# A fused attention, token-mixer and MLP kernel: the second batch's edges go, one rotation moves behind the first token unit, and the residual's transposing transfers lead

## The chip, the cores and the metric

One core of one Trainium2 chip runs the whole program. The metric is device time of one execution in microseconds (us). TensorE is the matrix engine, VectorE, ScalarE and GpSimd work on tiles in SBUF, and SyncE issues most of the transfers (DMAs). Each engine, and SyncE's queue with it, takes its instructions in the order in which they stand in the program; an instruction that waits holds up all that is behind it on its engine.

## The reference

Eight batches of 576 tokens and 512 channels (8 heads of 64) pass through three stages. Cut to what matters:

```python
kv  = einsum('bhsd,bhse->bhde', k, v)                 # per head, 64x64
out = einsum('bhsd,bhde->bhse', q, kv)
x   = out / sqrt(mean(out*out, -1) + 1e-6) * g_norm   # (B, S, 512)

theta = x @ w_theta                                   # rotation
y = w_tok_r @ (x * cos(theta)) + w_tok_i @ (x * sin(theta))
u = x + y
u = u + relu(u @ w_ch)

h = relu(u.T @ w_tok1) @ w_tok2                       # over tokens
u = u + h.T
return u + relu(u @ w_ch1) @ w_ch2                    # MLP, 1536 wide
```

## The kernel before

**Stages.** Every float32 product is made of three float16 products (`mm3`, L103 to L105): each operand is a high part and the low part that is left over. A batch's 576 tokens are five tiles, the last one of 64. For a batch the work is: `kv` (K units), `attend` (five a units, one a tile: product with q, square, sum, power on GpSimd, scaling to x, split into two halves xs, transposing transfer to xt, residual R), `rotate` (five r units: product with w_theta into pt, range reduction, sine and cosine, product with x into cs, split into zh and zl; the fifth, `rotate_last`, works the other way round and turns its result zt into the last two rows of zh by a transposing transfer, L450), `mix` (M00 to M03 for the first 256 token columns, M10 to M13 for the other 320; 27 matmuls each, the last three of which need zh's last two rows), `channel` (C00 to C13; after each second one a transposing transfer xt<-xs, L514), `token1` (H00, H01 on the first column chunk's xt; H10, H11 on the second's) and `token2` (T00 to T13). A K, a or r unit belongs to the next batch or the one after it, and is issued beside the M, C, H and T units of the current one. The second half of the program is the MLP over all batches, in eight pieces; its wide weights are decoded and prepared beside the batches (`stash`).

**What sets the order.** A list of names, `STEADY`, is the order of a batch's main units; a dictionary, `BESIDE`, says after which of them each r, a, load or weight unit is issued ("M12": "r2" issues the third tile's rotation after M12). A unit is a generator: `go` first steps every open unit by one `yield`, then starts the new one, so a unit's later operations stand in the program behind those of the units issued since. From this program order a scheduler makes each engine's order; it may move an instruction ahead where it counts the engine free. The helpers `lead` and `placed` (L77 and L81) limit it: `lead` notes the last instruction of a main unit on its engine, and `placed` adds an edge without a semaphore, so that a side operation does not stand ahead of the last noted one. `beside(o)` gives `placed` for every batch but the first, whose rotation has `early` (a higher priority) instead. So the attention of the second batch, issued beside the first batch's M units, stands on VectorE and ScalarE behind the evictions of those units (L476, L477). `decode` places its three VectorE operations likewise, also while the first batch is prepared.

Tile names: py is a mix product in PSUM, R the residual, uh and ul its halves, pr a channel product, ph a token product, pu its second, po an attention product, ss and ri the sum and its power. Two tiles of the name xs are shared by the halves xs and the last rotation's zt. There are 8 PSUM banks.

Of the kernel before, what the change touches and what calls it, by code (L numbers as in the profile page):

```python
# [14 lines left out]
ALU = mybir.AluOpType  # L15
# [13 lines left out]
def attn_mixer_kernel(  # L29
# [4 lines left out]
    nc = tc.nc  # L34
# [104 lines left out]
    wp = []  # L139

    def decode(val, raw):

        bits = val.bitcast(I32)
        first = nc.scalar.activation(val, raw[..., 1].bitcast(F32), AF.Copy, scale=2.0**-112)
        if wp:

            tc.keep_in_program_order(first)
        yield
        placed(nc.vector.tensor_scalar(bits, bits, 3, None, ALU.logical_shift_left))
        placed(nc.vector.scalar_tensor_tensor(bits, raw[..., 0], 29, bits, ALU.logical_shift_right, ALU.bitwise_or))  # L150
        placed(nc.vector.scalar_tensor_tensor(bits, raw[..., 1], -(2**31), bits, ALU.bitwise_and, ALU.bitwise_or))

    def weight(pool, w, src, part, n, hi, lo, scale, name, raw=None):

# [156 lines left out]
    def attend(o, r):  # L311

        b = o.b
        if r == 0:
            o.R = mp.tile([P, KD, S], F32, tag="R", name=f"R{b}", bufs=2)
            o.x, o.xt = {}, {}
        po = bank(f"po{b}{r}")
        for hp in range(HP):
            nc.tensor.matmul(po[:, hp * P:(hp + 1) * P], o.q[:, hp, r * P:(r + 1) * P], kvbd[:, hp, :], start=True, stop=True)
        po3 = po.rearrange("p (h d) -> p h d", d=D)  # L320
        ss = fp.tile([P, H], F32, tag="ss", name=f"ss{b}{r}", bufs=3)
        ri = fp.tile([P, H], F32, tag="ri", name=f"ri{b}{r}", bufs=3)
# [12 lines left out]
        nc.gpsimd.tensor_tensor(
            x3, ri.unsqueeze(2).to_broadcast([P, H, D]), gb.unsqueeze(1).to_broadcast([P, H, D]), ALU.mult
        )
        yield
        yield
        place(nc.vector.tensor_tensor(x3, po3, x3, ALU.mult))  # L340
        n = SR if r == NR else P
        R = o.R[:, :, r * P:r * P + n]
        if b == 0:

            yield
            px = bank(f"px{r}").rearrange("p (k t) -> p k t", k=KD)
            for kk in range(KD):
                nc.tensor.transpose(px[:, kk, :], x[:, kk * P:(kk + 1) * P], ident)
            yield
            split(xt[:, 0], xt[:, 1], px, 1.0)  # L350
            nc.scalar.activation(R, px[:, :, :n], AF.Copy, scale=SW)
            return
        if b > 1:
            yield
        place(nc.scalar.activation(xs[:, 0, :], x, AF.Copy))
        yield
        place(nc.vector.tensor_tensor(xs[:, 1, :], x, xs[:, 0, :], ALU.subtract))
        nc.sync.dma_start_transpose(xt.rearrange("p a k t -> p (a k) t"), xs.rearrange("p a d -> p (a d)"))
        for _ in range(3 if b > 1 else 2):
            yield  # L360
        place(nc.scalar.activation(R, xt[:, 0, :, :n], AF.Copy, scale=SW))
        yield
        place(nc.vector.scalar_tensor_tensor(R, xt[:, 1, :, :n], SW, R, ALU.mult, ALU.add))

    def beside(o):
        return placed if o.b else lambda ins: ins

    def prepare(o):
        if o.zh is None:
# [42 lines left out]
    def rotate_last(o, xt):  # L412
# [69 lines left out]
    def channel(o, c, ct):  # L482
# [25 lines left out]
        with urgent():  # L508
# [284 lines left out]
    def run(units, o, nxt, after, also):  # L793
# [23 lines left out]
    TOKENS1 = ["K00", "H00", "H01", "K10", "H10", "H11"]  # L817
    STEADY = MIX[:6] + CHANNEL[:2] + MIX[6:] + CHANNEL[2:4] + ["K00"] + CHANNEL[4:] + TOKENS1[1:] + TOKEN2
    BESIDE = {
        "M00": "a2", "M01": "a3", "M02": "a4 l w", "M03": "r0", "M11": "r1", "M12": "r2",  # L820
        "C03": "r4", "C10": "w", "H01": "r3 w", "H11": "n0", "T01": "n1 w", "T12": "w",
    }
    for b in range(B):
        loaded.clear()
# [23 lines left out]
        elif b == 1:  # L848
# [90 lines left out]
```

## Time and profile before

| what | value |
|---|---|
| time before, median of 3 runs | 1122.71 us (1122.53 to 1125.02) |
| the profiled execution, its own time | 1125.0 us |
| its span | 1123.2 us (1.8 us lie around it) |
| TensorE busy | 1072.1 us (95%) |
| TensorE weight loads busy | 814.7 us (73%) |
| VectorE / ScalarE / GpSimd busy | 829.7 / 560.1 / 229.3 us |
| TensorE's granted clock, mean | 0.983 |

The clock is a share of 2.4 GHz: 1.00 is that, 0.50 is 1.2 GHz. The timeline views list what each engine did, with the idle time before it and what ended that; SPq rows are issues of transfers on SyncE's queue. The first batch's own mixing ends near 116 us, the batches end at 625 us, and the rest is the MLP. One steady batch takes 71 to 74 us: the fourth (counted from zero, batch 3) has its H units at 344 to 360 us.

### The profile page before, as it was taken

Reading aid. Unit: us, or ns where it says so; the run is one execution under the profiler, and the core shown is the slowest. Engines: PE = TensorE matmul, PEld = TensorE weight load, DVE = VectorE, ACT = ScalarE, POOL = GpSimd, SP = SyncE. Lnnn points to the kernel's source line nnn. Section 1 sums busy time; section 2 is a strip of 40 time slices with the busy share of each in tenths; the row PEclk is TensorE's granted clock in tenths of the full one; section 3 lists DMA queues with packets and bytes.
Section 4 is the critical chain, followed back from the end, with each engine's and each line's share of the span. In section 5 each row is a group of like instructions: output and inputs, shape, how many; then the busy total and the mean of one; then the engine's idle time right before and its main releaser. Section 6 shows DMA issues by size and latency. Waiting matters only on the chain.

```text
span 1123.2 us, 21650 instructions
## 1 busy us (share of the span) xinstructions
PE 1072.1 (95%) x8884; PEld 814.7 (73%) x8884; DVE 829.7 (74%) x1475; ACT 560.1 (50%) x958; POOL 229.3 (20%) x290
## 2 busy tenths in 40 slices
PE   4786999999998999999999999999999999999998
PEld 3473767776875777667777777777777777777776
DVE  4978868888886987978836485858677585858584
ACT  3755635556455364564622454636364544546361
POOL 2405034372641925628000000000000000000000
PEclk9887999999998999999999999999999999999999
DMA  9535456875747647664284702020110102020101
GB/s 315 211 107 131 97 160 151 217 191 135 215 123 207 189 123 201 169 153 110 48 272 81 285 12 75 1 78 9 38 48 28 59 12 75 12 75 1 44 1 43
DMA packets 146611, 126.35 MB, mean 112 GB/s; under 512 B 93200, under 2 KB 123024, under 8 KB 146512
## 3 DMA queue, kind: packets, MB, share of 16 engines
q1 hardware_dynamic: 141136, 104.53, 34.0%
q0 software_dynamic: 5376, 20.45, 5.1%
q8 instruction: 69, 1.13, 0.4%
q14 instruction: 30, 0.25, 0.1%
HBM read 74.29 MB, written 29.88 MB: 93 GB/s over the span
## 4 chain that ended last, share of the span: by engine, by line
PE 61%; DVE 18%; DMA 8%; ACT 5%; issue 4%; POOL 3%; SPq 0%; ACTq 0%; DVEq 0%; POOLq 0%
PE na L103 4%; PE na L105 4%; PE pa L104 4%; PE pa L105 4%; PE na L104 4%; PE pa L103 4%; DMA xt<-xs 4%; DVE cs L403 2%; PE py L105 2%; PE py L103 2%; PE py L104 2%; PE nc L105 2%; PE pc L104 2%; PE pc L105 2%; PE pc L103 2%
## 5 line engine op out<-in xcount | busy, mean ns | idle before, releaser
L103 PE MATMUL py<-wmh,zh 128*128 128x320 f16 (+1 forms) x576 | 165.3, 287 | 0.7 <-DMA zh<-zt 0.5
L104 PE MATMUL py<-wml,zh 128*128 128x320 f16 (+1 forms) x576 | 165.0, 287 | 0.0
L105 PE MATMUL py<-wmh,zl 128*128 128x320 f16 (+1 forms) x512 | 146.5, 287 | 1.9 <-DVE zl L410 1.9
L105 PE MATMUL na<-gh,wbl 128*128 128x288 f16 x384 | 109.4, 286 | 0.0
L104 PE MATMUL pa<-o,wah 128*128 128x288 f16 x384 | 109.3, 286 | 0.0
L104 PE MATMUL na<-gl,wbh 128*128 128x288 f16 x384 | 109.2, 286 | 0.0
L103 PE MATMUL pa<-o,wah 128*128 128x288 f16 x384 | 108.4, 286 | 0.0
L105 PE MATMUL pa<-o,wal 128*128 128x288 f16 x384 | 107.8, 286 | 0.0
L103 PE MATMUL na<-gh,wbh 128*128 128x288 f16 x384 | 106.1, 286 | 0.2
L620 DVE TENSOR_TENSOR gl<-sum,gh 128x1152 f16<-128x1152 f32 x48 | 64.9, 1353 | 21.9 <-ACT gh L619 21.9
L104 PEld LDWEIGHTS <-wbh 128*128 128x128 f16 x672 | 65.7, 98 | 17.7 <-issue 0.9
L103 PEld LDWEIGHTS <-wah 128*128 128x128 f16 x672 | 65.7, 98 | 16.6
L104 PEld LDWEIGHTS <-wah 128*128 128x128 f16 x672 | 65.7, 98 | 16.6
L105 PEld LDWEIGHTS <-wbl 128*128 128x128 f16 x672 | 65.7, 98 | 16.6
L103 PEld LDWEIGHTS <-wbh 128*128 128x128 f16 x672 | 65.7, 98 | 16.6
L105 PEld LDWEIGHTS <-wal 128*128 128x128 f16 x672 | 65.7, 98 | 16.6
L334 POOL TENSOR_TENSOR ri<-ss,mhalf 128x8 f32<-128x8 f32 x40 | 76.8, 1920 | 1.6
L103 PE MATMUL pr<-uh,wch 128*128 128x256 f16 (+1 forms) x256 | 73.1, 286 | 0.0
L105 PE MATMUL pr<-uh,wcl 128*128 128x256 f16 (+1 forms) x256 | 73.0, 286 | 0.0
L104 PE MATMUL pr<-ul,wch 128*128 128x256 f16 (+1 forms) x256 | 73.0, 286 | 0.0
L103 PEld LDWEIGHTS <-zh 128*128 128x128 f16 x576 | 56.6, 98 | 16.8 <-DMA zh<-zt 0.9
L619 ACT ACTIVATE gh<-sum 128x1152 f16<-128x1152 f32 x48 | 55.5, 1156 | 25.5 <-DVE sum L667 25.5
(292 smaller groups left out, 2905.3 us busy)
## 6 DMA issues: line engine op xcount, KB each, us to landing
c<-u2d SPq DMA_DIRECT2D x32, 288.0 KB, 4.2
out<-c SPq DMA_DIRECT2D x64, 144.0 KB, 1.8
q<-in_q SPq DMA_DIRECT2D x7, 1152.0 KB, 8.5
k<-in_k SPq DMA_DIRECT2D x24, 256.0 KB, 5.7
v<-in_v SPq DMA_DIRECT2D x24, 256.0 KB, 5.8
wa_r<-in_w_ch SPq DMA_DIRECT2D x24, 256.0 KB, 3.6
wb_r<-in_w_ch SPq DMA_DIRECT2D x24, 256.0 KB, 3.9
wad<-wa POOLq DMA_DIRECT2D x24, 224.0 KB, 3.1
```

What stands on the lines that cost most here:

```text
L103: nc.tensor.matmul(acc, ah, bh, start=first and i == 0, stop=False, **more)
L104: nc.tensor.matmul(acc, ah, bl, start=False, stop=False, **more)
L105: nc.tensor.matmul(acc, al, bh, start=False, stop=last and i == n - 1, **more)
L334: nc.gpsimd.tensor_tensor(ri, ss, mhalf, ALU.pow)
L403: place(nc.vector.tensor_tensor(cs, cs, x.unsqueeze(1).to_broadcast([P, 2, DM]), ALU.mult))
L619: nc.scalar.activation(h.hi[:, 3:], h.s, AF.Copy)
L620: nc.vector.tensor_tensor(h.lo[:, 3:], h.s, h.hi[:, 3:], ALU.subtract)
```

## The change

Four edits. The second batch's side operations (batch 1 in the code) are no longer placed, so `beside` places only batches 2 to 7, and `decode` places nothing until the pool of stashed weights is open. The third tile's rotation r2 is issued after H00 and not after M12 (M13 in the second batch). L514's transfer becomes a leading one and those of attention (L358) and of the last rotation (L450) are placed behind it; for batches 2 to 7 the last one also comes three steps later.

```diff
 def decode(val, raw):
...
-        placed(nc.vector.tensor_scalar(bits, bits, 3, None, ALU.logical_shift_left))
+        place = placed if wp else lambda ins: ins
+        place(nc.vector.tensor_scalar(bits, bits, 3, None, ALU.logical_shift_left))
...
 def attend(o, r):
...
-        nc.sync.dma_start_transpose(xt..., xs...)
+        place(nc.sync.dma_start_transpose(xt..., xs...))
...
 def beside(o):
-        return placed if o.b else lambda ins: ins
+        return placed if o.b > 1 else lambda ins: ins
...
 def rotate_last(o, xt):
...
-            nc.sync.dma_start_transpose(o.zh[:, KM - 1:, :]..., zt...)
+        if b > 1:
+            for _ in range(3):
+                yield
+        place(nc.sync.dma_start_transpose(o.zh[:, KM - 1:, :]..., zt...))
...
 def channel(o, c, ct):
...
-                nc.sync.dma_start_transpose(xt[:, (ct - 1) * m:(ct + 1) * m, :], xsf)
+                lead(nc.sync.dma_start_transpose(xt[:, (ct - 1) * m:(ct + 1) * m, :], xsf))
...
 BESIDE = {
-        "M00": "a2", "M01": "a3", "M02": "a4 l w", "M03": "r0", "M11": "r1", "M12": "r2",
-        "C03": "r4", "C10": "w", "H01": "r3 w", "H11": "n0", "T01": "n1 w", "T12": "w",
+        "M00": "a2", "M01": "a3", "M02": "a4 l w", "M03": "r0", "M11": "r1",
+        "C03": "r4", "C10": "w", "H00": "r2", "H01": "r3 w", "H11": "n0", "T01": "n1 w", "T12": "w",
```

Line numbers of the changed kernel are one to five higher than the same lines before: L403 is L404 there, L476 is L481, L514 is L519.

**VectorE, end of the first batch's rotation.** Ahead of the first mix eviction (L476), before; zl is the low half of the rotated tiles, cs_513 and zt_514 are the last tile's:

```order
L403 TENSOR_TENSOR cs_446<-cs_446,x_293 128x1024
L410 TENSOR_TENSOR zl_224<-cs_411,zh_223 128x2x512
L410 TENSOR_TENSOR zl_224<-cs_446,zh_223 128x2x512
L431 SCALAR_TENSOR_TENSOR cs_513<-cs_513,pt_464 128x256
L442 SCALAR_TENSOR_TENSOR cs_513<-R_213,cs_513 128x4x64 x2
L449 TENSOR_TENSOR zt_514<-cs_513,zt_514 128x512
L476 TENSOR_TENSOR R_213<-py_623,R_213 128x256
L476 TENSOR_TENSOR R_213<-py_674,R_213 128x256
```
And now, from the same zl on (wc is the channel weight being decoded, x, ss and po the second batch's attention):

```order
L411 TENSOR_TENSOR zl_224<-cs_446,zh_223 128x2x512
L174 SCALAR_TENSOR_TENSOR wcl<-wc_0v,wch 128x512
L341 TENSOR_TENSOR x_716<-po_708,x_716 128x512
L432 SCALAR_TENSOR_TENSOR cs_513<-cs_513,pt_464 128x256
L333 TENSOR_REDUCE ss_833<-x_836 128x8
L151 SCALAR_TENSOR_TENSOR wc_1v<-wc_1r,wc_1v 128x512
L341 TENSOR_TENSOR x_775<-po_767,x_775 128x512
L443 SCALAR_TENSOR_TENSOR cs_513<-R_213,cs_513 128x4x64
L152 SCALAR_TENSOR_TENSOR wc_1v<-wc_1r,wc_1v 128x512
L443 SCALAR_TENSOR_TENSOR cs_513<-R_213,cs_513 128x4x64
L174 SCALAR_TENSOR_TENSOR wcl<-wc_1v,wch 128x512
L341 TENSOR_TENSOR x_836<-po_828,x_836 128x512
```
Sixteen operations of the second batch's attention (four ss, four x) and of two w_ch tiles (eight) now stand between the first batch's L403 and its zt; before, they all stood behind the evictions L476.

**SyncE's queue, C03 to the end of C13 of a steady batch.** xt_2822 and xt_3082 are the residual's two chunks, k and v the loads of a later batch, wa_r a stashed weight, zh the last rotation. Before:

```order
L267 DMA k_3074<-in_k 96x512
L267 DMA v_3076<-in_v 96x512
L267 DMA k_3078<-in_k 96x512
L514 DMA_TRANSPOSE xt_2822<-xs_2957 128x8x128
L267 DMA v_3080<-in_v 96x512
L137 DMA wa_r<-in_w_ch 128x2x256 x2
L514 DMA_TRANSPOSE xt_3082<-xs_3083 128x10x128
L450 DMA_TRANSPOSE zh_2707<-zt_3048 128x8x128
L514 DMA_TRANSPOSE xt_3082<-xs_3125 128x10x128
```
And now:

```order
L268 DMA k_3050<-in_k 96x512
L519 DMA_TRANSPOSE xt_2822<-xs_2940 128x8x128
L268 DMA v_3052<-in_v 96x512
L268 DMA k_3054<-in_k 96x512
L268 DMA v_3056<-in_v 96x512
L137 DMA wa_r<-in_w_ch 128x2x256 x2
L519 DMA_TRANSPOSE xt_3058<-xs_3059 128x10x128
L519 DMA_TRANSPOSE xt_3058<-xs_3103 128x10x128
L455 DMA_TRANSPOSE zh_2707<-zt_3027 128x8x128
```
The transfer of C03 stands ahead of three of four loads, and that of C13 ahead of the last rotation's.

**VectorE, the evictions of C02 and C03 of a steady batch.** cs_3726 is tile r1, cs_3830 tile r2, cs_3956 the last tile, wa_1 a stashed weight. Before:

```order
L410 TENSOR_TENSOR zl_3617<-cs_3726,zh_3616 128x2x512
L395 SCALAR_TENSOR_TENSOR cs_3830<-cs_3830,pt_3817 128x512
L480 SCALAR_TENSOR_TENSOR ul_3638<-R_2352,uh_3637 128x320
L502 SCALAR_TENSOR_TENSOR R_2352<-pr_3867,R_2352 128x256
L502 SCALAR_TENSOR_TENSOR R_2352<-pr_3889,R_2352 128x256
L510 SCALAR_TENSOR_TENSOR xs_3866<-R_2352,xs_3866 128x256
L238 SCALAR_TENSOR_TENSOR wa_1_3884<-wa_s,wa_0_3883 128x896
L510 SCALAR_TENSOR_TENSOR xs_3866<-R_2352,xs_3866 128x256
L431 SCALAR_TENSOR_TENSOR cs_3956<-cs_3956,pt_3907 128x256
L403 TENSOR_TENSOR cs_3830<-cs_3830,x_3446 128x1024
```
And now:

```order
L481 TENSOR_TENSOR R_2355<-py_3817,R_2355 128x320
L485 SCALAR_TENSOR_TENSOR ul_3638<-R_2355,uh_3637 128x320
L507 SCALAR_TENSOR_TENSOR R_2355<-pr_3850,R_2355 128x256
L411 TENSOR_TENSOR zl_3617<-cs_3726,zh_3616 128x2x512
L515 SCALAR_TENSOR_TENSOR xs_3849<-R_2355,xs_3849 128x256
L507 SCALAR_TENSOR_TENSOR R_2355<-pr_3867,R_2355 128x256
L515 SCALAR_TENSOR_TENSOR xs_3849<-R_2355,xs_3849 128x256
L239 SCALAR_TENSOR_TENSOR wa_1_3884<-wa_s,wa_0_3883 128x896
L432 SCALAR_TENSOR_TENSOR cs_3935<-cs_3935,pt_3886 128x256
L507 SCALAR_TENSOR_TENSOR R_2355<-pr_3969,R_2355 128x320
```
The range reduction, the product and the low half of r2 (L395, L403, L410 on cs_3830) are gone from here, and wa_1 stands behind C03's last operation. On TensorE r2's twelve matmuls moved from between M12 and M13 to between H00 and H01.

## Rows read from the trace of the kernel before

**Rows 1.** Busy time by stretch: engines in us (instructions), then clock, DMA share, GB/s.

```profile
78.00:118.00 40.00, 29.11 (x180) 18.33 (x179) 32.90 (x58) 20.77 (x40) 16.39 (x15) 0.83 0.40 99
324.00:395.00 71.00, 67.33 (x564) 47.65 (x562) 58.05 (x99) 35.64 (x65) 35.32 (x46) 0.95 0.61 167
620.00:1123.00 503.00, 499.70 (x4071) 397.91 (x4069) 340.64 (x616) 238.98 (x378) 1.42 (x2) 1.00 0.14 49
```

**Rows 2.** What TensorE waited for: us in total, times, the longest.

```profile
PE pt L103 <- DMA xt<-xs: 10.9, 1, 10.9
PE ph L530 <- DMA xt<-xs: 7.8, 9, 3.1
```

**Rows 3.** TensorE timeline, 60 to 104 us: start, length, operation, [idle before].

```profile
60.30 2.08 PE L319 MATMUL po<-kvbd,q 128*128 128x128 f32 x8
94.81 0.61 PE L103 MATMUL pt<-wth,xt 128*128 128x512 f16 x1 [10.89 <-DMA xt<-xs]
99.90 0.47 PE L103 MATMUL py<-wmh,zh 128*128 128x320 f16 x1
```

**Rows 4.** Busy time by stretch, three short stretches, for the clock.

```profile
96.00:98.00 2.00, 2.00 (x6) 0.76 (x5) 1.91 (x4) 0.67 (x1) 1.92 (x2) 0.50 1.05 217
280.00:284.00 4.00, 3.47 (x17) 1.68 (x18) 1.33 (x3) 1.89 (x4) 0.30 (x1) 1.00 0.95 283
354.00:358.00 4.00, 4.00 (x10) 1.36 (x9) 0.00 (x0) 0.58 (x1) 0.00 (x0) 0.50 0.93 275
```

**Rows 5.** VectorE's timeline, 60 to 85 us.

```profile
64.95 1.22 DVE L403 TENSOR_TENSOR cs<-cs,x 128x1024 f32<-128x1024 f32 x1
68.56 2.43 DVE L410 TENSOR_TENSOR zl<-cs,zh 128x1024 f16<-128x1024 f32 x2
73.90 0.69 DVE L449 TENSOR_TENSOR zt<-cs,zt 128x512 f16<-128x512 f32 x1 [0.70 <-ACT zt L446]
79.08 0.42 DVE L149 TENSOR_SCALAR wc_0v<-wc_0v 128x512 int32<-128x512 int32 x1
80.75 0.68 DVE L150 SCALAR_TENSOR_TENSOR wc_0v<-wc_0r,wc_0v 128x512 int32<-128x512 int32 x1
81.35 0.68 DVE L332 TENSOR_REDUCE ss<-x 128x8 f32<-128x512 f32 x1
```

**Rows 6.** ScalarE's timeline, 76 to 85 us.

```profile
79.19 0.58 ACT L330 ACTIVATE x<-po 128x512 f32<-128x512 f32 x1
```

**Rows 7.** Chain that ended last, 90 to 96 us: start, length, what.

```profile
91.66 3.10 DMA xt<-xs
```

**Rows 8.** TensorE's timeline at the first token mixing of two batches.

```profile
280.53 0.39 PE L530 MATMUL ph<-xt,w1h 128*128 128x512 f16 x1 [1.33 <-DMA xt<-xs]
343.95 0.38 PE L530 MATMUL ph<-xt,w1h 128*128 128x512 f16 x1 [0.61 <-DMA xt<-xs]
353.79 0.61 PE L530 MATMUL ph<-xt,w1h 128*128 128x512 f16 x1 [3.06 <-DMA xt<-xs]
```

**Rows 9.** SyncE's queue, 338 to 354 us.

```profile
340.00 1.26 SPq L514 DMA_TRANSPOSE xt<-xs  x1
348.78 1.25 SPq L450 DMA_TRANSPOSE zh<-zt  x1
350.14 1.36 SPq L514 DMA_TRANSPOSE xt<-xs  x1
```

**Rows 10.** VectorE's timeline, 332 to 350 us.

```profile
335.81 0.68 DVE L395 SCALAR_TENSOR_TENSOR cs<-cs,pt 128x512 f32<-128x512 f32 x1
338.55 1.09 DVE L238 SCALAR_TENSOR_TENSOR wa<-wa_s,wa 128x896 f16<-128x896 f32 x1 [0.41 <-ACT wa L236]
339.56 0.42 DVE L510 SCALAR_TENSOR_TENSOR xs<-R,xs 128x256 f16<-128x256 f32 x1
343.26 1.23 DVE L410 TENSOR_TENSOR zl<-cs,zh 128x1024 f16<-128x1024 f32 x1 [0.33 <-ACT zh L407]
```

**Rows 11.** TensorE's timeline at 565 us.

```profile
565.56 0.28 PE L103 MATMUL py<-wmh,zh 128*128 128x256 f16 x1 [0.45 <-DMA zh<-zt]
```

More of the change, by code (lines that the diff above doesn't have):

```diff
@@ L148, in decode @@
         yield
-        placed(nc.vector.tensor_scalar(bits, bits, 3, None, ALU.logical_shift_left))
-        placed(nc.vector.scalar_tensor_tensor(bits, raw[..., 0], 29, bits, ALU.logical_shift_right, ALU.bitwise_or))
-        placed(nc.vector.scalar_tensor_tensor(bits, raw[..., 1], -(2**31), bits, ALU.bitwise_and, ALU.bitwise_or))
+        place = placed if wp else lambda ins: ins
+        place(nc.vector.tensor_scalar(bits, bits, 3, None, ALU.logical_shift_left))
+        place(nc.vector.scalar_tensor_tensor(bits, raw[..., 0], 29, bits, ALU.logical_shift_right, ALU.bitwise_or))
+        place(nc.vector.scalar_tensor_tensor(bits, raw[..., 1], -(2**31), bits, ALU.bitwise_and, ALU.bitwise_or))
     def weight(pool, w, src, part, n, hi, lo, scale, name, raw=None):
@@ L357, in attend @@
         place(nc.vector.tensor_tensor(xs[:, 1, :], x, xs[:, 0, :], ALU.subtract))
-        nc.sync.dma_start_transpose(xt.rearrange("p a k t -> p (a k) t"), xs.rearrange("p a d -> p (a d)"))
+        place(nc.sync.dma_start_transpose(xt.rearrange("p a k t -> p (a k) t"), xs.rearrange("p a d -> p (a d)")))
         for _ in range(3 if b > 1 else 2):
@@ L449, in rotate_last @@
             place(nc.vector.tensor_tensor(zt[:, 1, :], sn, zt[:, 0, :], ALU.subtract))
-            nc.sync.dma_start_transpose(
-                o.zh[:, KM - 1:, :].rearrange("p i (k d) -> p (i k) d", k=KD), zt.rearrange("p i n -> p (i n)")
-        )
+        if b > 1:
+            for _ in range(3):
+                yield
+        place(nc.sync.dma_start_transpose(
+            o.zh[:, KM - 1:, :].rearrange("p i (k d) -> p (i k) d", k=KD), zt.rearrange("p i n -> p (i n)")
+        ))
     def mix(o, c, dt):
@@ L513, in channel @@
                 m = tiles + 2
-                nc.sync.dma_start_transpose(
-                    xt[:, (ct - 1) * m:(ct + 1) * m, :], xsf
-                )
+                lead(nc.sync.dma_start_transpose(xt[:, (ct - 1) * m:(ct + 1) * m, :], xsf))
     def token1(o, part, j):
@@ L853, in attn_mixer_kernel @@
             run(STEADY[STEADY.index("C01"):], o, nxt, after, {
-                "C01": "r0", "M12": "r1", "M13": "r2", "C03": "r4", "C10": "w", "H01": "r3 w", "H11": "n0", "T01": "n1 w", "T12": "w",
+                "C01": "r0", "M12": "r1", "C03": "r4", "C10": "w", "H00": "r2", "H01": "r3 w", "H11": "n0", "T01": "n1 w", "T12": "w",
             })
```

## Prediction

> **What bounds the kernel now.** I read the busy time by stretch first, because one mean hides stages with different limits. In the MLP half TensorE works 499.7 of 503 us at full clock [rows 1]; the change touches nothing there. Two stretches look different: from 78 to 118 us TensorE works 29 of 40 us at a granted clock of 0.83, and from 324 to 395 us 67.3 of 71 us at 0.95 [rows 1]. The list of TensorE's waits names both: once 10.9 us before a rotation (pt) for a transposing transfer xt, and nine times, 7.8 us together, before token matmuls (ph) for the residual's xt [rows 2]. So TensorE bounds the kernel, except where it waits for a transfer that was issued late. A wait costs twice if the clock falls: after the 10.9 us the next matmuls run at 0.50, 1.2 GHz [rows 4], and twelve rotation matmuls take 99.90 - 94.81 = 5.1 us [rows 3], half of it lost.
>
> **Edit 1, no edges in the second batch.** The product with q for its first tile ends at 62.4 us [rows 3], but its square was put behind the first mix evictions; it and its neighbours run from 79.2 us [rows 6], the sum follows at 81.35 [rows 5], and the transfer of that tile is issued only at 91.66 and lands 3.1 us later [rows 7]. TensorE meanwhile has nothing to do from 83.92 to 94.81 [rows 3]. In the new order sixteen VectorE operations go ahead of the first batch's zt. Their price: fourteen at 0.60 (the pitch from 80.75 to 81.35) and two at 0.42 at most [rows 5], 9.2 us. They cost something, since TensorE waits for what stands behind them. Eight of them (six at 0.60, two at 0.42: 4.4 us) stand ahead of the second zl, which ended at 70.99 [rows 5]; VectorE had no pause before that, so TensorE's mixing slides by 4.4 us and reaches the rotation at 83.9 + 4.4 = 88.3. The other end of the chain: zt ended at 74.6 [rows 5] and comes 9.2 later less the 1.7 us of pauses that it fills (the last, 0.70, is in rows 5), at 82.1; the first half xs follows 0.6 later, its transfer is issued behind zt's near 83.4, and at 3.1 us it lands at 86.5 [rows 7], or 2 us later if the two share the transfer engines. So TensorE's own lateness decides: the rotation starts at 88.3 and not at 94.8, 6.5 us, and the half clock behind the long wait goes too, 2.5 us. **-9.0 us.** After that VectorE has 32.9 us of work in these 40 [rows 1] less the 9.2 moved ahead, in some 26 us up to the channel units: tight, but room. The ends for this term: -13.4 if nothing were late (10.9 + 2.5), and -3 if the new wait brings the clock down (rival 1). I take the value between because each of its steps has a row.
>
> **Edit 2, r2 behind H00, and edit 3, the residual's transfers first.** The nine waits are four before H00, 2.2 us together (0.61 is one), and five before H10, 5.6 us together (3.06 and 1.33 are two) [rows 8]. In batch 3 TensorE reaches H10 at 350.7; the transfer of C13 is issued at 350.14, behind zt's at 348.78 [rows 9], and lands at 353.8, 3.6 us later. Now it leads, 1.4 us gained, and VectorE gets to it earlier by r2's range reduction, product and low part, 0.68 + 1.22 + 1.23 = 3.1 us [rows 5, 10]. It lands near 349.3, before TensorE asks. **The five waits before H10 go: -5.6 us.** Behind the 3.06 us the clock was 0.50 [rows 4]; 5% of 71 us [rows 1] is **-3.5 us**.
>
> What is late next is H00. Without r2's twelve matmuls (2.6 us at full clock) ahead, TensorE is there at 343.3 - 2.6 = 340.7 [rows 8]. C03's transfer waits for VectorE, whose operation ended at 339.98 [rows 10]; r2's 0.68 and the weight's 1.09 no longer stand ahead [rows 10], and I count 1.5 us of that. It took 3.9 us from its issue at 340.00 [rows 9] to H00's start, with loads ahead of it; two fewer now. 338.5 plus 3.1 [rows 7] to 3.9 is 341.6 to 342.4: a wait of 0.9 to 1.7 where it was 0.61. In the other batches VectorE was further ahead, so I leave this group at 2.2 us, **0**; its ends are -2.2 and +5.8 (five times 0.55 + 2.6 - 1.5).
>
> The price of r2's new place: its low part (1.23) stands between the two low parts of the token products, and the evictions of the T units behind it. TensorE has eight attention products and several T matmuls before it needs them, so I take 0.3 us a batch, **+1.5 us** for five; the ends are 0 and 6. SyncE's other transfers, the loads moved behind C03's, are needed one K unit later; nothing.
>
> **The last rotation's transfer** now stands behind C13's. In the steady batches zh's last rows are wanted a dozen units later: nothing. In the last batch TensorE already waits 0.45 us for them [rows 11]. The new order of matmuls puts some 8 us of other mixing ahead, about the delay of two transfers; **+0.5 us**, between -0.45 and +3.1, one transfer.
>
> **The sum.** 1125.0 (the profiled execution's own time: span 1123.2, 1.8 around it) - 9.0 - 5.6 - 3.5 + 1.5 + 0.5 = **1108.9 us**. That execution is 2.3 us above the median of 1122.71; its 3.06 us wait may be part of why, and since that wait is taken away I leave the sum where it is.
>
> **A rule that speaks against.** After the wait of 1.33 us the clock stayed at 1.00 in the stretch around it, and after 3.06 us it was 0.50 [rows 4]: short waits were free here. The Trainium skill (TensorE: Matmul & The Clock Gate, "A second HAM failure mode: psum-queue depth-cycling") says that frequent small idles between groups of matmuls are enough to make the clock swing between its two levels. By that the waits that stay before H00 would each be followed by slow matmuls; the trace agrees for the long one only. As a mechanism of this kernel: half clock in all five batches and not in one, five times 3.5 in place of none, 1108.9 + 17.5 = 1126 us. Chance 0.04.
>
> **Rivals.**
> 1. *The freed work hurts its host.* The 4.4 us that TensorE now waits near 70 to 75 us bring the clock to 0.50 as the long waits did, 2.5 us, and the transfers of zt and of the first tile queue up, up to 3.1 us more: the rotation starts near 93.9. Speaking for it: VectorE has almost no pause up to 71 us [rows 5]; against: the wait comes in two parts. 1108.9 + 5.6 = 1114.5. Chance 0.20.
> 2. *The wait only moves.* H00 waits for what H10 waited for, without loss of clock: the 5.6 us stay, 1114.5. For it: C03's transfer hangs on VectorE and not on the queue's order [rows 9, 10]. Chance 0.15. Both rivals together give 1120, chance 0.07.
> 3. *Slower.* Before H00, VectorE and the transfer come no earlier at all, so each of five batches waits 0.55 + 2.6 = 3.15 us there and the clock falls each time: the waits are 15.8 us where they were 7.8 (+8.0), the clock costs 17.5 where it was 3.5 (+14). 1125.0 - 9.0 + 8.0 + 14 + 2.0 = 1140. It decides somewhere between 1.33 and 3.06 us of wait [rows 4, 8]. Against it: the order shows two operations gone ahead of C03's. Chance 0.06.
>
> **How the numbers follow.** The forecast has 0.48, with a range of its own of 1105 to 1113. A measurement of this kernel can tell about 0.3% from no change, 3.4 us; faster means below 1119.3. That takes the forecast, rivals 1 and 2, and almost half of both together: 0.86. Within the bound lie the rest of that and half of the rule's case: 0.06; slower is rival 3 with the other half: 0.08. For 8 times in 10 the range goes from 1102 (the first term at its -13.4 end, H00's waits gone) to 1120.
>
> **What would show it.** Right: no wait of several us before the second batch's first rotation, which starts near 88 us, and waits of 1 to 4 us near 70 to 75 us; clock 1.00 from 88 us on; no H10 wait above 0.3 us; waits before H00 of 0 to 1.7 us; the first C00 some 9 us earlier. Wrong: H00 waits above 2 us with a clock of 0.50 behind them; a wait for zt's rows near 85 us; T evictions that hold TensorE for over 1 us a batch; more than 2 us of wait for zh in the last batch.

## Result and profile after

| | before | after |
|---|---|---|
| median of the runs (lowest to highest) | 1123.34 us (1122.53 to 1125.02) | 1129.22 us (1127.48 to 1132.28) |
| ratio, 95% interval | | 1.0060 (1.0038 to 1.0081) |
| profiled execution, its own time | 1125.0 us | 1127.48 us |
| TensorE's mean clock | 0.983 | 0.986 |

The change makes the kernel slower by 0.6%, 5.9 us by the medians. 1108.9 had been forecast, with 1102 to 1120 as the range. The two profiled executions are only 2.5 us apart, since that of before was the longest of its runs and that of after the shortest. What follows divides these 2.5 us and takes the size from the medians.

Windows of after (us, PE busy, PE loads, DVE, ACT, POOL, clock, DMA share, GB/s), the stretches of [rows 1] and four more:

```profile
78.00:118.00 40.00, 39.55 (x320) 27.83 (x318) 32.62 (x61) 24.08 (x46) 8.18 (x5) 1.00 0.48 106
118.00:160.00 42.00, 37.44 (x332) 27.77 (x331) 31.55 (x78) 19.05 (x43) 5.92 (x8) 0.96 0.59 156
250.00:324.00 74.00, 69.16 (x588) 49.58 (x586) 56.88 (x101) 37.89 (x68) 36.19 (x47) 0.98 0.64 168
324.00:395.00 71.00, 67.89 (x591) 49.52 (x590) 58.74 (x103) 37.24 (x66) 36.14 (x46) 1.00 0.68 178
395.00:466.00 71.00, 68.43 (x595) 49.86 (x593) 57.69 (x100) 38.36 (x68) 35.81 (x46) 1.00 0.70 171
466.00:537.00 71.00, 67.22 (x583) 48.75 (x581) 56.00 (x99) 38.56 (x69) 33.57 (x44) 1.00 0.52 121
620.00:1123.00 503.00, 501.79 (x4085) 399.46 (x4083) 341.69 (x617) 239.59 (x379) 1.42 (x2) 1.00 0.15 50
```

The stretch from 78 to 118 us is now full, 39.55 of 40 us at clock 1.00 against 29.11 at 0.83 [rows 1]. The MLP half is as it was, 501.79 us busy. The loss lies in between, and TensorE's waits say what it is (engine, line, what was waited for: us, times, longest):

```profile
PE ph L533 <- DMA xt<-xs: 5.4, 3, 2.5
PE pu L103 <- DVE R L550: 5.2, 5, 1.2
PE py L103 <- DMA zh<-zt: 3.1, 2, 2.7
PE ph L533 <- DVE xs L515: 3.0, 1, 3.0
PE py L103 <- ACT zh L408: 2.7, 1, 2.7
PE py L103 <- DVE R L550: 1.5, 5, 0.3
```

The 10.9 us before pt are gone [rows 2]. The token matmuls ph wait 5.4 + 3.0 = 8.4 us, where it was 7.8 us [rows 2], and all of it now stands before H00, none before H10. Two lines come back in each of five batches (1 to 5): the T units and the matmul behind them wait for an eviction (R from L550) that frees a PSUM bank, 5.2 + 1.5 = 6.7 us. TensorE's timeline at these places (start, us, idle before it):

```profile
87.73 0.39 PE L103 MATMUL pt<-wth,xt 128*128 128x512 f16 x1
...
133.39 0.39 PE L103 MATMUL py<-wmh,zh 128*128 128x256 f16 x1 [2.68 <-DMA zh<-zt]
...
216.99 0.27 PE L103 MATMUL py<-wmh,zh 128*128 128x256 f16 x1 [0.30 <-DVE R L550]
...
269.68 0.49 PE L533 MATMUL ph<-xt,w1h 128*128 128x512 f16 x1 [3.02 <-DVE xs L515]
...
291.43 0.30 PE L103 MATMUL pu<-w2h,hh 128*128 128x320 f16 x1 [0.99 <-DVE R L550]
293.53 0.27 PE L103 MATMUL py<-wmh,zh 128*128 128x256 f16 x1 [0.31 <-DVE R L550]
...
344.00 0.38 PE L533 MATMUL ph<-xt,w1h 128*128 128x512 f16 x1 [1.64 <-DMA xt<-xs]
...
512.06 0.27 PE L103 MATMUL py<-wmh,zh 128*128 128x256 f16 x1 [0.31 <-DVE R L550]
```

The rows at 216.99, 293.53 and 512.06 are the first matmuls (M00) of batches 2, 3 and 6. They divide the kernel. Batch 2 begins at 216.99 where it was 220.53: of the lead of 9.7 us that TensorE has at the first C00 (106.52 against 116.26), 3.5 is left. The four steady batches 2 to 5, from 216.99 to 512.06, take 295.1 us where they took 288.8 (220.53 to 509.33): 6.3 lost. What follows takes 615.4 us where it took 615.7. The sum is -3.5 + 6.3 - 0.3 = +2.5.

### The profile page after: what moved, and what is told of

Read it like the earlier page. It is cut to its first block, busy times and chain, and to the rows that moved or that the text cites. A ratio compares the mean times of both kernels' runs of the same rounds, so it can differ in the third digit from the quotient of the medians.

```text
span 1125.7 us, 21644 instructions
## 1 busy us (share of the span) xinstructions
PE 1073.4 (95%) x8884; PEld 815.4 (72%) x8884; DVE 822.9 (73%) x1475; ACT 561.0 (50%) x958; POOL 237.7 (21%) x290
## 4 chain that ended last, share of the span: by engine, by line
PE 61%; DVE 16%; DMA 8%; ACT 7%; POOL 4%; issue 3%; SPq 1%; ACTq 0%; POOLq 0%; DVEq 0%
PE na L103 4%; PE na L105 4%; PE na L104 4%; PE pa L105 4%; PE pa L104 4%; PE pa L103 4%; DMA xt<-xs 3%; DVE cs L404 2%; PE nc L104 2%; PE nc L103 2%; PE pc L105 2%; PE pc L104 2%; PE pc L103 2%; PE nc L105 2%; PE py L103 2%
## 5 line engine op out<-in xcount | busy, mean ns | idle before, releaser
L103 PE MATMUL py<-wmh,zh 128*128 128x256 f16 (+1 forms) x576 | 166.2, 289 | 7.3 <-DMA zh<-zt 3.1
L104 PE MATMUL py<-wml,zh 128*128 128x256 f16 (+1 forms) x576 | 166.4, 289 | 0.0
L105 PE MATMUL pa<-o,wal 128*128 128x288 f16 x384 | 107.8, 286 | 0.0
L335 POOL TENSOR_TENSOR ri<-ss,mhalf 128x8 f32<-128x8 f32 x40 | 73.5, 1838 | 2.0
L103 PEld LDWEIGHTS <-zh 128*128 128x128 f16 x576 | 57.0, 99 | 21.9 <-DMA zh<-zt 3.6
L104 PEld LDWEIGHTS <-zh 128*128 128x128 f16 x576 | 57.0, 99 | 18.0 <-issue 2.5
```

The source lines that it names most:

```text
L103: nc.tensor.matmul(acc, ah, bh, start=first and i == 0, stop=False, **more)
L104: nc.tensor.matmul(acc, ah, bl, start=False, stop=False, **more)
L105: nc.tensor.matmul(acc, al, bh, start=False, stop=last and i == n - 1, **more)
```

## Experiments

Three theories: **theory 1**, moving r2 behind H00 (edit 2) is the cost; **theory 2**, the new order of the transfers (edit 3) is; **theory 3**, what edit 1 gains is lost in the stretch behind it, whatever else is done. "M00" is where batch 2's mixing starts in the profiled execution, "four" the time of batches 2 to 5, as above; both are of one execution, and M00 alone spreads from 219.1 to 221.6 among the kernels without edit 1.

| kernel | median us | ratio to before (95%) | M00 | four |
|---|---|---|---|---|
| before | 1123.34 | 1 | 220.5 | 288.8 |
| after (1+2+3) | 1129.22 | 1.0060 (1.0038 to 1.0081) | 217.0 | 295.1 |
| edit 1 | 1119.64 | 0.9974 (0.9960 to 0.9987) | 216.5 | 286.3 |
| edit 2 | 1132.69 | 1.0094 (1.0073 to 1.0115) | 221.2 | 294.2 |
| edit 3 | 1118.58 | 0.9966 (0.9949 to 0.9982) | 219.8 | 281.2 |
| 1+3 | 1115.92 | 0.9943 (0.9922 to 0.9964) | 216.3 | 282.0 |
| 1+3, last rotation earlier | 1115.91 | 0.9925 (0.9908 to 0.9941) | 218.9 | 281.2 |
| 1 (attention only)+3 | 1113.35 | 0.9905 (0.9885 to 0.9925) | 217.7 | 281.6 |
| after, r1 doubled | 1134.28 | 1.0097 (1.0072 to 1.0123) | 219.2 | 295.7 |
| 1+3, r2 behind C10 | 1117.95 | 0.9945 (0.9923 to 0.9967) | 213.9 | 287.7 |
| after, r2's zl on GpSimd | 1122.41 | 0.9987 (0.9972 to 1.0001) | 217.8 | 288.1 |
| lead and place only | 1123.55 | 0.9999 (0.9984 to 1.0015) | 221.6 | 287.1 |
| three steps only | 1123.34 | 1.0006 (0.9991 to 1.0021) | 219.1 | 286.6 |

**The edits apart.** Edit 1:

```diff
-        return placed if o.b else lambda ins: ins
+        return placed if o.b > 1 else lambda ins: ins
+        place = placed if wp else lambda ins: ins
-        placed(nc.vector.tensor_scalar(bits, bits, 3, None, ALU.logical_shift_left))
+        place(nc.vector.tensor_scalar(bits, bits, 3, None, ALU.logical_shift_left))
```

> Kernel before with edit 1 alone: the second batch's side operations and the first weights' decoding are not placed. Theory 1 (r2 behind H00 is what costs): the wait of 10.9 us before the second batch's first rotation goes, the rotation starts near 88 us, and of the 9.7 us that the first C00 gains 7 to 9 reach the end: 1115. Theory 2 (the new order of the transfers is what costs): the same, 1115, and no wait of several us near 133 us for zh, since the last rotation's transfer is where it was. Theory 3 (edit 1's gain is swallowed by the stretch behind it, whatever the other edits do): C00 comes some 9 us earlier, but the second batch's own M00 at 220 us no more than 2 us: 1121 to 1123.

Measured: 1119.64, and M00 of batch 2 at 216.5, 4.0 earlier. The first C00 came at 107.8, 8.5 earlier, so more than half of the gain is lost between C00 and M00, and theories 1 and 2 were 4.6 us too low with their 1115. The wait for zh near 134 us stands here too (2.69 us), with the transfers as they were in the program: theory 2 does not explain it. Theory 3's M00 is refuted, its point stands in half.

Edit 2 alone:

```diff
-        ... "M03": "r0", "M11": "r1", "M12": "r2",
-        "C03": "r4", "C10": "w", "H01": "r3 w", ...
+        ... "M03": "r0", "M11": "r1",
+        "C03": "r4", "C10": "w", "H00": "r2", "H01": "r3 w", ...
```

> Kernel before with edit 2 alone: r2 behind H00, the transfers as they were. Theory 1: the H10 waits go (5.6 us) and the half clock in batch 3 (3.5 us), but H00 waits of 2 to 3 us come in five batches and token2 waits 1 to 1.4 us for PSUM in each: 1127 to 1131, with batches of 73 to 75 us. Theory 2: near the time of before or a little under it, 1119 to 1123. Theory 3: the steady batches lose what they lose in the whole change, 5 to 6 us: 1128.

Measured: 1132.69, four batches 294.2. H00 waits of 2.94, 1.84, 1.32 and 2.03 us and the same five waits for evictions (6.1 us); before H10 only 0.45 us is left. Theory 1's terms are all there, a little dearer than expected.

Edit 3 alone:

```diff
-        nc.sync.dma_start_transpose(xt..., xs...)
+        place(nc.sync.dma_start_transpose(xt..., xs...))
...
+        if b > 1:
+            for _ in range(3):
+                yield
-            nc.sync.dma_start_transpose(o.zh..., zt...)
+        place(nc.sync.dma_start_transpose(o.zh..., zt...))
...
-                nc.sync.dma_start_transpose(xt..., xsf)
+                lead(nc.sync.dma_start_transpose(xt..., xsf))
```

> Kernel before with edit 3 alone: the residual's transposing transfers lead, those of attention and last rotation are placed behind them, and the last rotation's comes three steps later; r2 stays behind M12. Theory 1: the H10 waits shrink by up to 1.4 us each, nothing else: 1117 to 1123. Theory 2: a wait of 2 to 3 us for zh with half clock behind it near 140 us in the second batch, and waits in the others: 1127 to 1132. Theory 3: 1121 to 1124.

Measured: 1118.58, four batches 281.2 and not 288.8. The waits of ph for a transfer are 2.2 us in two places, with r2 where it was. Theory 2 falls: this edit is a gain.

Edits 1 and 3 together (the two diffs above), r2 left behind M12:

> The changed kernel without edit 2: no edges in the second batch and the new order of transfers, r2 behind M12 as before. Theory 1: edit 1's gain is kept: 1111 to 1116. Theory 2: the 2.7 us wait for zh at 133 us stays with its half clock, and more waits in the steady batches: 1122 to 1130. Theory 3: 1120 to 1123.

Measured: 1115.92, the two gains nearly added (-3.3 and -4.3 alone, -7.0 together). Adding edit 2 to this makes 1129.22: **edit 2 costs 13.3 us**, the whole loss and the other two gains besides. Alone it costs 9.8 (1132.69 against 1122.89 beside it); the difference is likely the waits before H10, which edit 2 and edit 3 each take away and which can be gained only once. (Each median of before that was taken beside a group of runs lies between 1122.89 and 1124.30.)

**Why r2 costs there: H00.** VectorE around C03 of batch 2 in the changed kernel (start, us, what; its C03 product ended at 256.71 on TensorE):

```profile
258.17 1.22 DVE L404 TENSOR_TENSOR cs<-cs,x 128x1024 f32<-128x1024 f32 x1
...
259.71 0.48 DVE L481 TENSOR_TENSOR R<-py,R 128x320 f32<-128x320 f32 x1
...
261.67 1.23 DVE L411 TENSOR_TENSOR zl<-cs,zh 128x1024 f16<-128x1024 f32 x1
...
263.15 0.42 DVE L507 SCALAR_TENSOR_TENSOR R<-pr,R 128x256 f32<-128x256 f32 x1
264.05 0.42 DVE L515 SCALAR_TENSOR_TENSOR xs<-R,xs 128x256 f16<-128x256 f32 x1 [0.48 <-ACT xs L508]
...
284.44 1.22 DVE L411 TENSOR_TENSOR zl<-cs,zh 128x1024 f16<-128x1024 f32 x1
285.57 1.22 DVE L404 TENSOR_TENSOR cs<-cs,x 128x1024 f32<-128x1024 f32 x1
...
289.83 1.22 DVE L411 TENSOR_TENSOR zl<-cs,zh 128x1024 f16<-128x1024 f32 x1
290.96 0.75 DVE L550 SCALAR_TENSOR_TENSOR R<-pu,R 128x256 f32<-128x256 f32 x2
```

And with edits 1 and 3 only, where C03's product ended at 258.63 (L506 is L507, L514 is L515, L549 is L550 there):

```profile
257.73 1.23 DVE L411 TENSOR_TENSOR zl<-cs,zh 128x1024 f16<-128x1024 f32 x1
...
259.87 0.75 DVE L506 SCALAR_TENSOR_TENSOR R<-pr,R 128x256 f32<-128x256 f32 x2
...
262.62 0.42 DVE L514 SCALAR_TENSOR_TENSOR xs<-R,xs 128x256 f16<-128x256 f32 x1
...
283.92 0.41 DVE L549 SCALAR_TENSOR_TENSOR R<-pu,R 128x256 f32<-128x256 f32 x1
```

C03's low half ends 264.47 - 256.71 = 7.8 us behind its product in the changed kernel and 263.04 - 258.63 = 4.4 with r2 behind M12. TensorE runs ahead by r2's 2.75 us, and VectorE comes no earlier for it: counted from M00, C03's low half ends at 47.5 us here and at 46.7 there. It takes up M13's product 5.6 us after its end (254.09 to 259.71; with r2 behind M12 1.2 us, 256.02 to 257.19), and r1's low half (L411) now stands between the evictions of C02 and C03. If so, TensorE has time to give away there:

```diff
-        mm3(pt, [...])
+        for _ in range(2 if r == 1 and b > 1 else 1):
+            mm3(pt, [...])
```

> The changed kernel with the twelve matmuls of r1 done twice in batches 2 to 7 (the first twelve are overwritten by the second): 2.75 us more TensorE work in each, ahead of C02 and C03, and nothing more for any other engine. Theory 1 (with r2 gone, TensorE reaches H00 2.75 us earlier than VectorE and the transfer can follow): the H00 waits of 1.3 to 3.0 us shrink to under 0.7 and take up most of it: of 6 x 2.75 = 16.5 us, 13.8 of it in the five batches that wait or not, 5 to 9 reach the end: 1134 to 1138. Rival (H00's wait comes from the transfers or from VectorE operations that stand right ahead of the low half, whatever TensorE does): all of it reaches the end, 1143 to 1146, with the H00 waits unchanged.

Measured: 1134.28, but the four batches take 295.7 where they took 295.1. **11.0 us of added matmuls (four times 2.75) cost 0.6 us.** One H00 wait of 0.8 is left where 8.4 us were:

```profile
PE pu L103 <- DVE R L551: 5.7, 5, 1.6
...
PE ph L534 <- DMA xt<-xs: 0.8, 1, 0.8
```

VectorE goes by its own time: C03's low half ends 46.2 to 47.3 us behind M00, against 46.1 to 47.5 without the added matmuls, although its product comes 2.6 us later. The 0.6 is a sum: the batch that had the wait of 3.02 us and the half clock behind it is 2.2 us shorter, the other three are 0.2 to 1.5 us longer each. The remaining 5 us arise outside the four batches, in those before and after, where nothing waits at H00. So r2's matmuls behind M12 were nearly free cover, and the change took them away.

**Why r2 costs there: the T units.** From the first T matmul of batch 2 to the next M00, first after, then edits 1 and 3 only:

```profile
285.10:293.50 8.40, 7.13 (x58) 5.61 (x58) 8.40 (x13) 3.26 (x5) 5.28 (x7) 1.00 0.34 127
```
```profile
279.40:286.20 6.80, 6.80 (x59) 5.61 (x57) 6.22 (x12) 3.44 (x5) 2.96 (x4) 1.00 0.88 311
```

VectorE works 8.40 of 8.40 us, and the first eviction starts at 290.96, 5.2 us after the end of the first T product, behind L411 twice and L404 (rows above). Taking one of them away:

```diff
-            place(nc.vector.tensor_tensor(zl[:, at, :], cs, zh[:, at, :], ALU.subtract))
+            low = nc.gpsimd if r == 2 and b > 1 else nc.vector
+            place(low.tensor_tensor(zl[:, at, :], cs, zh[:, at, :], ALU.subtract))
```

> The changed kernel with one VectorE operation of r2, the low half zl (1.22 us), done on GpSimd in batches 2 to 7. Theory 1 (in the T units VectorE has work for all of the 8.4 us, and the first eviction stands behind two operations of r2 and r3): the waits for an eviction, 1.0 and 0.3 us in each of five batches, shrink below 0.4 together: 1122 to 1126. Rival (it is the order of the evictions or the banks, not VectorE's load): they stay, 1128 to 1131; or GpSimd's slower operation makes the mixing wait for zl, 1130 or more.

Measured: 1122.41, 6.8 below the changed kernel; the waits for evictions fall from 6.7 to 3.0 us, ph's from 8.4 to 4.9 (3.7 for a transfer, 1.2 for VectorE). They are 0.5 to 1.0 a batch, above theory 1's 0.4, but the rival's "they stay" is refuted: one operation of 1.2 us a batch decides half of edit 2's cost, since VectorE is the bound there.

A place in between, with edits 1 and 3:

```diff
-        ... "M11": "r1", "M12": "r2",
-        "C03": "r4", "C10": "w", ...
+        ... "M11": "r1",
+        "C03": "r4", "C10": "r2 w", ...
```

> Edits 1 and 3, with r2 issued after C10, four units ahead of H00. Theory 1 (two causes: TensorE's cover ahead of C02 and C03 is gone, and VectorE carries r2 and r3 between H00 and the T units): the twelve matmuls stand between C03 and H00 and hide C03's transfer, so H00 waits are under 0.5, and the evictions of the T units wait 0 to 0.6 us: 1114 to 1121. Rival (any place behind C03 costs the same, since VectorE's work is what moved): T units wait 1 us or more and H10 waits 1 to 3 us for C13: 1124 to 1130.

Measured: 1117.95. Against the kernel before beside it that is 0.9945, as with r2 behind M12 (0.9943): no difference clear of noise, though the four batches are 5.7 us longer. No waits for evictions and none at H00, as theory 1 had it, but H10 waits in all four batches, 1.08, 2.01, 3.38 and 0.60 us; behind the longest the clock is 0.50:

```profile
417.80:420.00 2.20, 2.20 (x6) 0.82 (x7) 0.41 (x1) 1.19 (x2) 0.32 (x1) 0.50 0.88 217
```

The wait goes to whichever transfer VectorE feeds last. The rival was half right: C13's low half pays now.

**What in edit 3 gains.** First `lead` and `place` without the three steps, then the three steps without them:

```diff
-        if b > 1:
-            for _ in range(3):
-                yield
```

> Kernel before with edit 3 but without the three steps by which the last rotation's transfer comes later: the residual's transfers lead and the others are placed, no more. Theory 1 (what the edit gains is the residual's place in SyncE's queue): H10 waits as with the whole edit, 1.3 us at most: 1117 to 1120. Rival (the three steps are what puts zh's transfer behind C13's): H10 waits of 1 to 3 us in most batches: 1121 to 1124.

Measured: 1123.55, no gain; H10 waits up to 2.8 us.

```diff
+        if b > 1:
+            for _ in range(3):
+                yield
         nc.sync.dma_start_transpose(o.zh..., zt...)
```

> Kernel before with the three steps by which the last rotation's transfer comes later, in batches 2 to 7, and nothing else of edit 3: no leading and no placed transfers. Theory 1 (the steps put zh's transfer behind C13's in SyncE's queue, and that is the whole gain of the edit): H10 waits of 1.3 us at most, 1117 to 1120. Rival (steps and leading transfers are needed together, since without the noted order the scheduler moves zh's transfer ahead again): H10 waits of 1 to 3 us as before, 1121 to 1124.

Measured: 1123.34, no gain either; H10 waits up to 2.6 us. SyncE's queue in batch 3 shows it: with the whole edit (L517 is the residual's, L453 zt's), C11's and C13's transfers stand together ahead of zt's,

```profile
343.55 3.61 SPq L517 DMA_TRANSPOSE xt<-xs  x2
347.21 1.40 SPq L453 DMA_TRANSPOSE zh<-zt  x1
```

with lead and place alone,

```profile
346.72 2.32 SPq L514 DMA_TRANSPOSE xt<-xs  x1
349.14 1.25 SPq L450 DMA_TRANSPOSE zh<-zt  x1
350.50 1.39 SPq L514 DMA_TRANSPOSE xt<-xs  x1
```

and with the steps alone (L519 and L455)

```profile
345.34 2.15 SPq L519 DMA_TRANSPOSE xt<-xs  x1
347.59 1.25 SPq L455 DMA_TRANSPOSE zh<-zt  x1
348.95 1.37 SPq L519 DMA_TRANSPOSE xt<-xs  x1
```

zt's is between them as before [rows 9]. Neither the later place in the program nor the edge holds it back by itself; likely the edge goes to C11's transfer where zt's comes early in the program, and without an edge the scheduler moves zt's ahead again. Each half is worth nothing, together they are worth 4.3 us.

**Where edit 1's other half goes.** In every kernel with edit 1 the second batch's mixing waits for zh near 133 us. Its last two rotations two units earlier:

```diff
-    ... "M13": "w",
+    ... "M13": "r3 w",
...
-    "C00": "w", "C01": "r3 w", "C02": "w", "C03": "r4 w", ...
+    "C00": "w", "C01": "r4 w", "C02": "w", "C03": "w", ...
```

> Edits 1 and 3 with the second batch's last two rotations issued two units earlier (r3 after M13, r4 after C01). Theory 1: the wait of 2.6 us for zh at 133.7 us, which stands in every kernel with edit 1, comes from a transfer of the last rotation that is issued only behind C03, while the mixing now arrives 9 us earlier; it goes, with 1.6 us of half clock behind it: 1111 to 1113, the second batch's M00 at 212 to 213 us. Rival: VectorE and the queue's weight loads are what is late there (VectorE is busy 14.7 of the 15.7 us before): the wait stays or moves to zl or to the first C units, 1115 to 1117.

Measured: 1115.91; the wait stays, 3.34 us: the rival. The last rotation's matmuls ended at 112.7, 3.4 us earlier than with edits 1 and 3, but ScalarE, busy with other work for 5.3 of the 5.9 us between, took up their result only at 118.6, 2.0 earlier.

Without the part of edit 1 that frees the decoding (against edits 1 and 3):

```diff
-        place(nc.vector.tensor_scalar(bits, bits, 3, None, ALU.logical_shift_left))
+        placed(nc.vector.tensor_scalar(bits, bits, 3, None, ALU.logical_shift_left))
```

> Edits 1 and 3 without the part of edit 1 that frees the decoding of w_ch: its VectorE operations are placed as before, only the attention is freed. Theory 1 (the freed operations are paid by the host, 2.5 us of wait for zh at 67.8 and 2.2 us for po at 71, with the clock at 0.61 to 0.70 up to 78 us): without the eight decoding operations these waits shrink by half, C00 comes at 104 to 105 and the end at 1113. Rival: the attention's own eight operations make the waits, or the weights wc come later and the channel units wait for them: C00 at 107 to 110, 1116 to 1120.

Measured: 1113.35, the expected end by another way. The waits near 68 to 71 us fall to 1.8 and 0.7, but C00 is where it was, 106.8; the wait for zh is 0.9 us, and 2.2 us of waiting for the copied row weights take its place. The same with those weights loaded earlier:

```diff
-extra += [weight_tile(wp[0], w_tok1, w1, j, ...) for j in range(NR)]
+extra += [weight_tile(wp[0], w_tok1, w1, j, ...) for j in range(2)]
 extra += [weight(wp[0], w_tok1, src[SM:], SR, DT, w1rh[:SR], w1rl[:SR], SW, "w1r")]
+extra += [weight_tile(wp[0], w_tok1, w1, j, ...) for j in range(2, NR)]
```

> Edits 1 (attention only) and 3, with the short last tile of w_tok1 loaded and decoded ahead of its third and fourth tiles. Theory 1 (after the zh wait shrank to 0.9 us, the first batch's H10 waits 2.2 us for the copied rows of that tile, with the clock at 0.64 behind): the wait goes and some of the half clock with it: 1110 to 1112. Rival (VectorE, which decodes all of them and is busy 13.2 of 13.5 us before, is what is late): the same matmuls wait for another tile of w_tok1 instead: 1113 to 1115.

Measured: 1113.85 (0.9906, 0.9881 to 0.9931): that wait goes and others come (1.05 for hl, 1.97 for kvbd): the rival's time, by other waits than it named. Then VectorE's load, by giving the second batch's zl to GpSimd, with edits 1 and 3 and with edit 1 for the attention only:

```diff
+            low = nc.gpsimd if b == 1 else nc.vector
-            place(nc.vector.tensor_tensor(zl[:, at, :], cs, zh[:, at, :], ALU.subtract))
+            place(low.tensor_tensor(zl[:, at, :], cs, zh[:, at, :], ALU.subtract))
```

> Edits 1 and 3, with the second batch's four low halves zl (1.22 us each on VectorE) done on GpSimd, which has 5.6 us of work from 88 to 133.7 us. Theory 1 (VectorE's 41.4 us of work in these 45.7 us give edit 1's gain back): the last rotation's chain ends earlier, the wait of 2.6 us for zh and the 1.6 us of half clock behind it shrink by half or more, 1111 to 1114. Rival (the transfer's own time and the weight loads ahead of it): the wait stays at 2.4 us or more, 1115 to 1117; or the mixing waits for zl, which takes 2.1 us on GpSimd.

> The same with edit 1 for the attention only and edit 3, whose zh wait was 0.9 us, with 2.2 us before H10 for the row weights. Theory 1: the zh wait goes, and the first batch's token units, which hang on VectorE's decoding too, wait less: 1109 to 1112. Rival: 1113 to 1115, as without it.

Measured: 1115.63 (0.9921, 0.9899 to 0.9943) and 1112.85 (0.9895, 0.9870 to 0.9920), their intervals overlap those of the same kernels without it. In the first the mixing waits 1.93 us for zh and, as the rival had it, 1.81 for zl on GpSimd; in the second the wait for zh grew from 0.9 to 2.74. They tell nothing of VectorE, since it was not relieved. GpSimd and VectorE in the first of the two:

```profile
118.64 2.13 POOL L412 TENSOR_TENSOR zl<-cs,zh 128x1024 f16<-128x1024 f32 x1 [4.55 <-ACT zh L408]
```
```profile
118.65 0.42 DVE L507 SCALAR_TENSOR_TENSOR R<-pr,R 128x256 f32<-128x256 f32 x1
118.99 2.06 DVE L174 SCALAR_TENSOR_TENSOR w1l<-w_0v,w1h 128x256 f16<-128x256 f32 x1
```

An operation of 0.42 us took 2.06 while GpSimd worked. So work was left out instead:

```diff
+        if wp and val.shape[-1] == 2 * P:
+            return
         place(nc.vector.scalar_tensor_tensor(bits, raw[..., 0], 29, ...))
```

> Edits 1 and 3, with two of the three VectorE operations that decode each tile of w_tok1 left out (the lowest bits and the signs; the token product then works with other weights, of the same sizes). Six of these ten operations, some 2.2 us, stand ahead of the second batch's zt on VectorE. Theory 1 (VectorE's work is what gives edit 1's gain back): zt and its transfer come about 2 us earlier, the wait of 2.6 us for zh shrinks to under 1 us and the 1.6 us of half clock behind it go: the second batch's M00 at 213 to 214 us and 1111 to 1114. Rival (the transfer's way through the queue, behind loads that now come earlier too): the wait stays at 2 us or more, 1115 to 1117.

Measured: 1113.35 (0.9906, 0.9888 to 0.9924), M00 of batch 2 at 214.6. The time is theory 1's, the mechanism is not: the wait for zh is 3.19 us, and the gain lies behind it, between 149 and 215 us. Nor was VectorE relieved much: from 106.7 to 129.4 us it is busy 20.09 us, with edits 1 and 3 it was 20.85, since later operations came forward; zt ends 0.3 us earlier and not 2. What sets that wait is left open.

**A version that beats both**: edit 1 for the attention only, edit 3, r2 behind M12: 1113.35 us, 0.9905 of before. Whether it beats edits 1 and 3 whole (0.9943, 0.9922 to 0.9964) is not shown; its interval (0.9885 to 0.9925) touches theirs.

## Why the prediction was wrong

Most of the miss lies in the four batches, in two steps: VectorE was taken to come earlier at H00 once r2 was gone, and its work behind H00 was not added up. A smaller part is edit 1, whose gain was followed to the first C00 only.

1. *Edit 1, -9.0.* Up to the first C00 the figures held: pt starts at 87.73 where 88.3 was forecast, the clock is 1.00 from 78 to 118 us, C00 comes 9.7 us earlier. One step on the way did not. The half clock did not go, it moved: from 67 to 78 us, around the waits of 2.7 and 1.8 us that replace the long one, the clock is 0.69 where it was 1.00 (after, then before),

```profile
67.00:78.00 11.00, 8.26 (x52) 6.65 (x53) 11.00 (x16) 5.81 (x10) 10.53 (x10) 0.69 0.00 0
67.00:78.00 11.00, 10.22 (x92) 8.63 (x91) 5.85 (x8) 5.08 (x9) 0.00 (x0) 1.00 0.13 24
```

which is the first half of rival 1. That 88.3 was met all the same is partly luck: from 56 to 67 us the clock was 0.69 before and is 0.84 now, which the forecast did not have. The step that failed comes behind "tight, but room": VectorE's work was counted up to the channel units only, and the sum takes the gain at the rotation for a gain at the end, with nothing for the second batch's zt. From C00 to zt's issue VectorE is busy 21.80 of 23.4 us in the changed kernel,

```profile
106.50:129.90 23.40, 22.93 (x223) 18.16 (x220) 21.80 (x47) 17.95 (x36) 0.00 (x0) 1.00 0.28 66
```

and in the kernel before

```profile
116.30:135.70 19.40, 19.40 (x191) 15.24 (x190) 18.52 (x43) 15.15 (x32) 0.00 (x0) 1.00 0.39 86
```

So 3.3 us more of its work stand there, zt's transfer is 135.70 - 129.88 = 5.8 us earlier and not 9.7, and TensorE waits 2.68. That VectorE's load is the cause is argued from these rows; no run shows it, and ScalarE may have a part too (the run with the last rotation earlier). Measured alone the edit gives -3.3 us.
2. *The five H10 waits, -5.6.* They went, in batch 3 for the reason given: counted from M00, C13's transfer is issued at 54.4 us where it was 58.5, 2.5 us of that VectorE's and the rest the lead. Two things were not in it. The lead does this only together with the three steps, which were read as a matter of zh alone. And TensorE comes to H10 later, by 0.6 to 5.1 us, since it waits at H00 and does r2 ahead of H10: edit 2 alone leaves 0.45 us of these waits.
3. *H00, 0 with ends of -2.2 and +5.8* (by its own numbers the upper end is 8.25 - 2.2 = 6.05). It was 8.4 against 2.2, +6.2, outside its ends. In batch 3, from which it was read, it held: 1.64 us, with 0.9 to 1.7 forecast. The step that failed is "in the other batches VectorE was further ahead, so I leave this group": TensorE comes to C03's end 2.6 us earlier in every batch, but VectorE, for which 1.5 us was counted, hardly moves. Counted from M00, C03's low half ended at 46.7, 48.3, 46.4 and 46.7 us in batches 2 to 5 and ends at 47.5, 46.2, 46.1 and 46.5 now, so the waits are 3.02, 1.64, 1.33 and 2.47 us. Taking an operation from a list does not move the rest up by its length when other operations slide into its place; r1's low half did. Rival 2 (the wait only moves from H10 to H00) is what happened to this group: 7.8 us became 8.4.
4. *T units, +1.5 with ends of 0 and 6.* 6.7 us, outside the ends, mis-sized by 5.2. The step that failed is TensorE's matmuls taken as cover without adding up VectorE's work behind H00, which fills the T units.
5. *Clock in batch 3, -3.5.* It is 1.00 there now, right, but the wait of 3.02 us brings it down in batch 2. Less its waits a batch takes 69.6 us before and 69.7 now; batch 3 before (76.1 from M00 to M00) has 72.5 and batch 2 now 71.9. So the half clock cost 2.9 us, not 3.5, and 2.2 of it came back.
6. *Last batch, +0.5.* No wait for zh is left there, -0.45: the lower end.

By stretches the sum leaves nothing over. Up to M00 of batch 2 the forecast has -8.7 (edit 1, and 0.3 for the first T units) and the runs -3.5; in the four batches -7.9 against +6.3; behind them +0.5 against -0.3. 1108.9 + 5.2 + 14.2 - 0.8 = 1127.5, the profiled execution's time. The 14.2 are H00 (6.2), T units (4.1 in these four), the clock (2.9) and about 1 of small waits. Rival 3 named the right side and half the mechanism, VectorE no earlier at H00, but priced it by waits of 3.15 us with half clock in every batch; only one wait was that long. No rival had the T units. Of the signs named for "wrong", three came: an H00 wait above 2 us with half clock behind it, a wait for zt's rows near 85 us (0.45), and T evictions that hold TensorE for over 1 us a batch.

## What to carry over

Matmuls on the bounding engine can be nearly free cover for an engine that trails it: before moving them, sum the trailing engine's work between the two places, up to the next point at which it is waited for, and test with doubled matmuls. Follow a gain at the start to the next transfer that it does not bring forward. The order in SyncE's queue needed both here, a later place in the program and an edge that holds it there.

## What was unexpected of the hardware

GpSimd and VectorE did not always work side by side. Beside a GpSimd operation of 2.13 us VectorE's L174 took 2.06 in place of 0.42 (rows above), and beside the next one L152, 0.42 elsewhere, took 2.28:

```profile
125.00 2.28 DVE L152 SCALAR_TENSOR_TENSOR w_1v<-w_1r,w_1v 128x256 int32<-128x256 int32 x1
```

Both read two tiles in SBUF. L507, which reads one of its two (pr) from PSUM, kept its 0.42 us inside the same GpSimd operation (118.65). The Trainium skill (GPSIMD Engine Reference, "1. Specifications") says that the two share their SBUF interfaces and contend when VectorE's instruction has two SBUF inputs; these rows agree. Where the same operation fell into a pause of VectorE (282.23 us in the kernel with r2's zl on GpSimd), only a copy with one input stood beside it, 0.43 us long, and nothing was held.

The clock does not follow the length of a wait alone. Behind waits of 1.33, 1.64 and 2.47 us before H00 it stayed at 1.00, behind 3.02 it was 0.54. But behind 2.48 before H10 (edit 1 alone) it was 0.62, behind 2.57 (three steps only) 1.00, and behind 2.19 (attention only) 0.50. The Trainium skill (TensorE: Matmul & The Clock Gate, "A second HAM failure mode: psum-queue depth-cycling") says that frequent small idles between groups of matmuls can make the clock swing. The trace of the kernel before agrees in one place: behind waits of 1.33, 0.51 and 1.29 us near 56, 57 and 60 us the clock is 0.50 (59.90 to 61.90 us). The steady batches do not test it: batches 3 to 5 of the changed kernel have three waits in some 72 us each, at a clock of 1.00.
